# An RWKV attention with a Fourier mix: mirrored row blocks of the fourth batch share their products, x is reversed through DRAM, and the order is written anew

## The chip, the core and the metric

The kernel runs on one core of a Trainium2 chip. The metric is device microseconds of one execution, as a median of several. The engines are TensorE (PE; PEld is its weight load), VectorE (DVE), ScalarE (ACT), GpSimd (POOL) and SyncE (SP, which issues most of the DMAs).

## The reference

Four batches, 768 positions, 8 heads of 48 columns, so d_model is 384. First a linear attention with a decaying state, then a mixing block.

```python
for t in range(S):                       # state: [B, H, 48, 48]
    cur = np.einsum('bhd,bhe->bhde', u[None] * kt, vt)
    y[:, :, t] = np.einsum('bhd,bhde->bhe', rt, state + cur)
    state = wt[:, :, :, None] * state + np.einsum('bhd,bhe->bhde', kt, vt)
x = y, heads side by side                # [4, 768, 384]
mixed = real(fft(fft(x, axis=1), axis=2))
u = x + mixed
un = (u - mean(u)) / sqrt(var(u) + 1e-06)        # per row
out = u + maximum(un @ w_ch1, 0) @ w_ch2         # 384 -> 1536 -> 384
```

The real part of the two transforms has a symmetry: row 768 - t of `mixed`, read backwards over the columns 1 to 383, is row t.

## The kernel before, in words

**Tiling.** Each batch has 6 chunks of 128 rows. `attention` (from L981) works a chunk: it takes the logarithm of w, sums it along the rows with triangular masks on TensorE (L1019; for the first batch, whose chunks go in pairs, L863), makes decayed r and k, transposes them, forms score blocks (L1130, 8 matmuls for a chunk), masks them (L1140) and sums values (L1195); `xb` gets the chunk's x (L1206). `fold` (L1222) adds and subtracts x rows and columns, so that the transform along the sequence needs half the products.

**The mix.** `mix` (L1256) works one batch. TensorE forms the sequence transform for 385 of the rows into `hcs` (L1271, an eviction for each of three column blocks j = 0, 2, 1); the other rows are the mirror of these and are written to `HCR` as a reversed copy with a sign (from L1298). Then each of six row blocks kb gets its products with the column table: `whole` (L1317) takes 3 matmuls with a 384-column table DTM, `parts` (L1326) takes 4 matmuls of 193, 193, 191 and 191 columns and puts the halves together with more vector work. A choice u(b, kb) says how x is added: from the bank by VectorE with `whole` (L1347), by a ScalarE copy and an addition, or with `parts` (L1362, L1365). Then come row statistics (L1376, L1378) and the centred rows `un` as bf16. Three blocks make a half. Its transposition is a choice too: `un_pe` (L1388: 9 transposes on TensorE, L1394, and evictions) or `un_dma` (L1400: one transposing DMA on SP). Then W1 with 12 groups of three matmuls (L1426), relu (L1432 on VectorE, L1434 on ScalarE), W2 with 12 matmuls for a row block (L1446), the result with its residual (L1455), and the write (L1466). The last row block of the fourth batch is split into 256 and 128 columns.

**The start.** `early` (L1477) runs 16 matmuls on a filled part of W1's tile (fill L613); then come the bonus row's matmuls (L713) and, when NW is not 0, NW matmuls on constants (L1522). On ScalarE: the sine tables with one activation table, a load of another (L762), the copy of the bonus row, then the logarithms of the first two chunk pairs. The weights come by POOL's DMAs (W1 at L822, W2 at L827).

**What sets the order.** All operations are first recorded with numbers. `ORDER` lists for each engine the numbers in the order in which the engine issues them; an operation that stands on one of several lists runs on that engine, and a choice is made by listing the operations of one way. `schedule` (L231) follows the lists and gives out PSUM banks, and `emit` (L342) adds semaphore waits. Each engine works its list in order; a waiting operation holds up those behind it, on SP and POOL their DMA issues too. At the end VectorE waits for all writes of the output.

Of the kernel before, what the change touches and what calls it, by code (L numbers as in the profile page):

```python
# [34 lines left out]
NW = 9  # L35

MEANS = (0,)

# [28 lines left out]
    "act": (  # L67
# [15 lines left out]
    "dve": (  # L83
# [17 lines left out]
    "pool": (  # L101
# [49 lines left out]
class _Prog:  # L151
# [190 lines left out]
    def emit(self):  # L342
# [57 lines left out]
        def run(name, eng):  # L400
# [8 lines left out]
            if name == "dve":  # L409
                for s in dcount:  # L410
                    if s.startswith("out"):
                        eng.wait_ge(sems[s], dcount[s])
# [1143 lines left out]
```

## Time and profile before

| | us |
|---|---|
| median of 3 runs (177.77 to 178.5) | 177.8 |
| the profiled execution | 177.74 |
| its span | 175.9 |
| busy: PE / PEld | 171.5 / 114.4 |
| busy: DVE / ACT / POOL | 156.0 / 130.9 / 104.9 |

The span is what the profile shows of one execution; the rest of the time lies around it. Busy times are sums over the span; matmuls are pipelined and their ends are modelled. The chain of waits is followed back from the last instruction.

### The profile page before, as it was taken

Reading aid. Unit: us, or ns where it says so; the run is one execution under the profiler, and the core shown is the slowest. Engines: PE = TensorE matmul, PEld = TensorE weight load, DVE = VectorE, ACT = ScalarE, POOL = GpSimd, SP = SyncE. Lnnn points to the kernel's source line nnn. Section 1 sums busy time; section 2 is a strip of 40 time slices with the busy share of each in tenths; the row PEclk is TensorE's granted clock in tenths of the full one; section 3 lists DMA queues with packets and bytes.
Section 4 is the critical chain, followed back from the end, with each engine's and each line's share of the span. In section 5 each row is a group of like instructions: output and inputs, shape, how many; then the busy total and the mean of one; then the engine's idle time right before and its main releaser. Section 6 shows DMA issues by size and latency. Waiting matters only on the chain.

```text
span 175.9 us, 4537 instructions
## 1 busy us (share of the span) xinstructions
PE 171.5 (97%) x1691; PEld 114.4 (65%) x1691; DVE 156.0 (89%) x374; ACT 130.9 (74%) x320; POOL 104.9 (60%) x145
## 2 busy tenths in 40 slices
PE   6999999999999999999999999999999999999994
PEld 3456767867766667766666667666666776666663
DVE  7999999999999999999999999999899599826253
ACT  2899999999999895999997888797841772454010
POOL 4025279779999466799996929998388334000000
PEclk9999999999999999999999999999999999999999
DMA  5999999899999999999699799969981104240033
GB/s 151 319 270 256 179 216 198 157 178 194 194 180 210 187 207 189 229 237 190 127 202 196 156 204 209 235 88 266 212 203 45 45 6 112 75 130 0 0 134 134
DMA packets 109031, 29.55 MB, mean 168 GB/s; under 512 B 104273, under 2 KB 109010, under 8 KB 109010
## 3 DMA queue, kind: packets, MB, share of 16 engines
q1 hardware_dynamic: 107394, 26.91, 71.8%
q0 software_dynamic: 1616, 2.36, 8.5%
q8 instruction: 13, 0.21, 0.5%
q14 instruction: 8, 0.07, 0.1%
HBM read 23.59 MB, written 4.72 MB: 161 GB/s over the span
## 4 chain that ended last, share of the span: by engine, by line
PE 81%; ACT 14%; DVE 2%; issue 1%; ACTq 0%; DVEq 0%
PE bank L1446 27%; PE bank L1426 27%; PE bank L1317 5%; PE bank L1271 4%; ACT rkt L625 3%; PE bank L1130 3%; PE bank L1195 2%; PE bank L1119 2%; PE bank L998 2%; PE bank L1192 2%; PE bank L1167 1%; ACT vb L616 1%; ACT uf L892 1%; ACT in_w L888 1%; ACT uf L616 1%; PE bank L1019 1%
## 5 line engine op out<-in xcount | busy, mean ns | idle before, releaser
L1426 PE MATMUL bank<-unt,w 128*128 128x384 bf16 x288 | 54.0, 326 | 0.0
L1446 PE MATMUL bank<-w,ht 128*128 128x384 bf16 (+2 forms) x300 | 52.7, 320 | 0.0
L1434 ACT ACTIVATE ht<-bank 128x384 bf16<-128x384 f32 x75 | 35.0, 509 | 13.6 <-PE bank L1426 13.4
L1446 PEld LDWEIGHTS bank<-w,ht 128*128 128x128 bf16 x300 | 27.8, 98 | 15.8 <-DVE ah L1140 0.2
L1426 PEld LDWEIGHTS bank<-unt,w 128*128 128x128 bf16 x288 | 26.8, 98 | 15.2
L1140 DVE TENSOR_TENSOR ah<-bank,msk 128x512 bf16<-128x512 f32 x47 | 30.3, 678 | 0.4 <-PE bank L1130 0.2
L1432 DVE TENSOR_SCALAR ht<-bank 128x384 bf16<-128x384 f32 x21 | 11.2, 552 | 7.7 <-PE bank L1426 7.7
L1455 DVE SCALAR_TENSOR_TENSOR osb<-bank,rstd,uf 128x384 f32<-128x384 f32 (+2 forms) x23 | 13.4, 591 | 4.7 <-PE bank L1446 2.6
L625 ACT ACTIVATE rkt<-bank 128x512 bf16<-128x512 bf16 (+1 forms) x22 | 16.4, 796 | 0.9 <-PE bank L1107 0.7
L602 POOL TENSOR_TENSOR xf<-sd 128x382 bf16<-128x382 f32 (+1 forms) x11 | 10.8, 1002 | 10.2 <-DVE sd L602 7.5
L616 ACT ACTIVATE un<-uf,agg 128x384 bf16<-128x384 f32 x22 | 13.1, 613 | 4.9 <-DVE agg L1378 4.9
L602 POOL TENSOR_TENSOR rkh<-in_k,e 128x384 bf16<-128x384 f32 x15 | 15.0, 1006 | 2.4 <-DVE rk L602 1.5
L602 POOL TENSOR_TENSOR rk<-in_r,in_k 128x384 f32<-128x384 f32 x14 | 13.9, 1002 | 0.8 <-DVE vtd L602 0.8
L602 POOL TENSOR_TENSOR vtd<-in_v,dc 128x384 f32<-128x384 f32 x17 | 14.2, 835 | 0.4 <-DVE dc L1074 0.3
L602 POOL TENSOR_TENSOR rk<-rk,ub 128x384 f32<-128x384 f32 x13 | 13.0, 1005 | 2.0 <-DVE rk L602 2.0
L616 ACT ACTIVATE vb<-in_v 128x384 bf16<-128x384 f32 x23 | 12.9, 569 | 1.2 <-DMA in_v<-in_v_dram 1.2
L1195 PE MATMUL bank<-vb,ah 128*128 128x48 bf16 x192 | 11.2, 183 | 0.0
L1206 DVE TENSOR_TENSOR x<-bank,vtd 128x384 f32<-128x384 f32 x19 | 10.4, 547 | 0.8 <-PE bank L1195 0.7
L1195 PEld LDWEIGHTS bank<-vb,ah 128*128 128x128 bf16 x192 | 9.7, 96 | 1.1 <-issue 0.2
L616 ACT ACTIVATE lb<-in_w 128x384 bf16<-128x384 f32 x18 | 9.7, 542 | 0.1
L1376 DVE BATCH_NORM_STATS2 bst<-uf 128x6 f32<-128x384 f32 x18 | 9.5, 546 | 0.2 <-POOL uf L602 0.2
L1192 PE MATMUL bank<-st,rkt 128*128 128x96 bf16 x80 | 9.7, 204 | 0.0
(208 smaller groups left out, 391.3 us busy)
## 6 DMA issues: line engine op xcount, KB each, us to landing
in_v<-in_v_dram SPq DMA_DIRECT2D x24, 192.0 KB, 3.9
out_dram<-osb SPq DMA_DIRECT2D x23, 192.0 KB, 2.3
in_r<-in_r_dram SPq DMA_DIRECT2D x18, 192.0 KB, 4.2
in_w<-in_w_dram SPq DMA_DIRECT2D x18, 192.0 KB, 3.8
in_k<-in_k_dram SPq DMA_DIRECT2D x18, 192.0 KB, 3.8
in_k<-in_k_dram SPq DMA_DIRECT2D x3, 384.0 KB, 4.5
in_r<-in_r_dram SPq DMA_DIRECT2D x3, 384.0 KB, 4.5
in_w<-in_w_dram SPq DMA_DIRECT2D x3, 384.0 KB, 4.6
```

Of the source, the lines that this page charges most:

```text
L602: return lambda e: e.tensor_tensor(out=o, in0=a, in1=b, op=f)
L616: return lambda e: e.activation(o, a, f, **kw)
L625: {"act": lambda e: e.activation(o(), i(), ACTF.Copy), "dve": lambda e: e.tensor_copy(out=o(), in_=i())}, **kw)
L1140: masked[n].append(op("dve", v_1(512), lambda e: e.tensor_tensor(out=ah[:, x:H:2, :], in0=ps(bk)[:, :].rearrange("p (h t) -> p h t", t=128 ...
L1192: e.matmul(ps(ty)[:, 96 * q:96 * q + 96], rT[:, q, :], s_in[:, q, :], start=not ype, stop=False, skip_group_check=True)
L1195: ins = e.matmul(ps(ty)[:, D * h:D * h + D], ah[:, h, :], vb[:, h, :], start=first and not ype, stop=True, skip_group_check=True)
L1206: op("dve", v_1(DM), lambda e: e.tensor_tensor(out=xb[:, c, 0:DM], in0=ps(ty)[:, 0:DM], in1=vflat, op=ALU.add), r=[ty, ("VTD", n % 4)], w= ...
L1426: ins = e.matmul(ps(t)[:, 0:384], W1[:, m, 256 * (j // 2) + j % 2:256 * (j // 2) + 256:2], unt[:, :, m, :], start=(m == 0), stop=(m == NM ...
L1432: {"dve": lambda e, j=j, t=t, ht=ht: e.tensor_scalar(out=ht[:, j, :], in0=ps(t)[:, 0:384], scalar1=su, scalar2=0.0, op0=ALU.mult, op1=ALU. ...
L1434: "act": lambda e, j=j, t=t, ht=ht: e.activation(ht[:, j, :], ps(t)[:, 0:384], ACTF.Relu, scale=su)},
L1446: ins = e.matmul(ps(t)[:, 0:hi - lo], ht[:, j, 128 * x:128 * x + 128], W2[:, j, lo:hi], start=(j == 0), stop=(j == NJ - 1))
L1455: op("dve", v_1(hi - lo) + 64, lambda e: e.scalar_tensor_tensor(out=o[:, lo:hi], in0=ps(t)[:, 0:hi - lo], scalar=rstd[:, kb:kb + 1], in1=u ...
```

## The change

- `NW` goes from 9 to 0: the matmuls on constants (L1522) are gone.
- `MIRROR = (3,)`: in the fourth batch (b = 3) `HCR` gets 128 reversed columns for each j, and one more copied column, in place of 384. Six row blocks remain, in this order: rows 0 to 127; 128 to 255; 640 to 767; 256 to 383; and then the mirrors of the fourth and of the second, read backwards out of the bank that holds those (`back_bank`), without matmuls. These two banks have 385 columns in place of 384, for which the table DTM gets a column more.
- The mirrored blocks need x with its rows reversed: three SP DMAs write rows 384 to 640 of x to a DRAM scratch `xs3`, and two indirect DMAs on POOL read them back by an index tile `IXI`, made by two iotas on POOL at the start. In the block of row 640 the first row is replaced by row 384 (one column of `HCR`, one row of `xb`); row 640 itself comes with the mirror of the block 128 to 255.
- The results of the mirrored blocks leave by two indirect DMAs on POOL (scatters), which wait for the write of rows 640 to 767; row 384 has its own small write. In the second half the blocks come out in the order 4, 5, 3, and block 3 is the one that is split into 256 and 128 columns.
- VectorE's last waits take in the semaphore of that small write.
- `ORDER` is new for every engine. In it, u(3,0) is `parts`, u(3,1) to u(3,3) are `whole` with VectorE's addition, u(3,4) and u(3,5) are `back_bank`; the first half's transposition of the fourth batch is `un_pe` (before `un_dma`), the second half's stays `un_dma`; one sum of the third batch takes the way with one cumulative matmul (L1019) fewer; the score blocks stand in 18 runs (17 before). The fill for the first 16 matmuls is VectorE's 11th operation (before its first). ScalarE has the first pair's logarithm ahead of the copy of the bonus row. Between the engines, 21 operations go from POOL to VectorE, 14 from VectorE to POOL, 11 from VectorE to ScalarE, 8 from ScalarE to VectorE; the first copy of values goes from ScalarE to POOL. Up to the third of VectorE's table operations (L610) there are 24 operations on its list (before 27). On SP the writes of x to the scratch stand between result writes of the second and third batch; POOL's list ends with the fold, the two gathers, one reversal, one addition and the two scatters.

```diff
-NW = 9
+NW = 0
+MIRROR, T_IND = (3,), 1100
...
-                    if s.startswith("out"):
+                    if s.startswith(("out", "one")):
                         eng.wait_ge(sems[s], dcount[s])
...
-    DTM = sb("dtm", [3, DM], BF16)
+    DTM = sb("dtm", [3, DM + 2], BF16)
+    IXI = sb("ixi", [4], mybir.dt.int32)
...
+        op("pool", 100, lambda e: e.iota(IXI[:, 0:2], [[-128, 2]], base=256, channel_multiplier=-1), w=["IXI"])
+        op("pool", 100, lambda e: e.iota(IXI[:, 2:4], [[128, 2]], base=S * (B - 1) + 512, channel_multiplier=-1), w=["IXO"])
...
+            if b in MIRROR:
+                some = lambda j=j: (HCR[:, j, 256:384], hcs[:, j, 128:0:-1])
...
+        if b in MIRROR:
...
+            xs = XS[b]
+            for q, (lo, n) in enumerate(((0, 128), (128, 128), (256, 1))):
+                op("sp", 620, lambda e, q=q, lo=lo, n=n: e.dma_start(xs[lo:lo + n, :], xb[0:n, 3 + q, 0:DM]),
+                   r=[("X", i, 3 + q)], w=[("XS", b, q)], sem="xs%d_%d" % (b, q), xfer=520 if n > 1 else 100, dma=(1150, 850))
...
+            for y in range(2):
+                op("pool", T_IND, lambda e, y=y: e.indirect_dma_start(
+                    xb[:, 4 - y, 0:DM], None, xs[:, :], bass.IndirectOffsetOnAxis(ap=IXI[:, y:y + 1], axis=0)),
+                   r=[("XS", b, q) for q in range(3 - y)] + ["IXI"], w=[("X", i, 4 - y)], sem="xr%d_%d" % (b, y), xfer=600, dma=(1150, 1300))
...
+            twin, back = mir and kb in (1, 3), mir and kb in (4, 5)
+            row = (0, 128, 256 + 384, 256, 0, 0)[kb] if mir else 128 * kb
+            xk = (0, 1, 5, 2, 3, 4)[kb] if mir else kb
+            t = banks[{4: 3, 5: 1}[kb]] if back else g.tile("f")
...
+                def back_bank(kb=kb, t=t, xk=xk):
+                    op("dve", v_1(DM), lambda e: e.tensor_tensor(
+                        out=uf[:, kb, :], in0=ps(t)[:, DM:0:-1], in1=xb[:, xk, 0:DM], op=ALU.add),
+                       r=[t, ("X", i, xk)], w=[("UF", i, kb)])
...
-                for lo, hi in ((0, DM),) if n < B * NC - 1 else ((0, 256), (256, DM)):
+                for lo, hi in ((0, DM),) if n != B * NC - (3 if B - 1 in MIRROR else 1) else ((0, 256), (256, DM)):
...
+                        if kb > 3:
+                            op("pool", T_IND, lambda e, o=o, kb=kb: e.indirect_dma_start(
+                                out.rearrange("b t d -> (b t) d"), bass.IndirectOffsetOnAxis(ap=IXI[:, kb - 2:kb - 1], axis=0), o[:, :], None),
+                               r=[("OSB", n % 3, lo), "IXO", ("out", b, 2, 0)], w=[("out", b, kb, lo)], sem="outs%d_%d" % (b, kb), xfer=600,
+                               dma=(1150, 1300))
+                            continue
```

## Rows read from the trace of the kernel before

**Rows 1.** The page's busy times: us, share of span, instructions

```profile
PE 171.5 (97%) x1691; PEld 114.4 (65%) x1691; DVE 156.0 (89%) x374; ACT 130.9 (74%) x320; POOL 104.9 (60%) x145
```

**Rows 2.** The chain that ended last, its share of the span by engine

```profile
PE 81%; ACT 14%; DVE 2%; issue 1%; ACTq 0%; DVEq 0%
```

**Rows 3.** Chain of waits in time, 6 to 31 us: start us, us, engine, tile, line

```profile
6.52 1.29 ACT L762
...
8.38 1.47 ACT uf L616 x2
...
11.04 0.41 ACT vb L616
...
29.33 0.94 ACT lb L616 x2
...
30.32 0.34 PE bank L1019
```

**Rows 4.** Windows: length, sum, busy PE, PEld, DVE, ACT, POOL (instructions), PEclk, DMA share, GB/s

```profile
40.00:60.00 20.00, 20.00 (x239) 13.86 (x238) 19.67 (x46) 20.00 (x55) 18.11 (x25) 1.00 1.03 189
...
120.00:140.00 20.00, 20.00 (x189) 13.39 (x188) 17.25 (x36) 12.36 (x32) 12.29 (x13) 1.00 0.72 153
```

**Rows 5.** Timeline, first 10 us: start us, us, engine, line, operation, shape

```profile
1.32 5.30 PE L1479 MATMUL bank<-w 128*128 128x384 bf16 x16 [1.32 <-DVE w L613]
...
7.48 1.64 PE L1522 MATMUL bank<-idw,msk 128*128 128x384 bf16 x9
...
9.26 2.11 PE L863 MATMUL bank<-uf,un 128*128 128x384 bf16 x12
...
1.30 0.11 DVE L613 MEMSET lb<- 128x64 uint32 x1
```

**Rows 6.** Chain of waits, 141 to 150 us

```profile
141.35 0.33 PE bank L1317 x2
...
142.98 0.50 PE bank L1326 x6
...
144.30 0.49 PE bank L1426 x3
...
144.78 5.20 PE bank L1446 x32
```

**Rows 7.** Windows, 139 to 146 us, L1326 alone: busy PE and PEld

```profile
139.00:146.00 7.00, 2.47 (x16) 1.44 (x16) 1.00 0.01 4
```

**Rows 8.** Chain of waits, 105 to 118 us

```profile
105.99 0.33 PE bank L1130 x8
...
114.08 0.22 PE bank L1119 x4
...
117.49 0.55 PE bank L1130 x16
```

**Rows 9.** Timeline of VectorE, batch 3 x sums and additions

```profile
134.81 0.55 DVE L1206 TENSOR_TENSOR x<-bank,vtd 128x384 f32<-128x384 f32 x1
...
141.71 0.56 DVE L1347 TENSOR_TENSOR uf<-bank,x 128x384 f32<-128x384 f32 x1
```

**Rows 10.** DMAs: L827 issue ns; landings of L827, L822, last L1466; transposing DMAs, median

```profile
L827 POOL DMA_DIRECT2D w<-in_moe_w_ch_dram x3: 742/753/757, 44.5 to 56.6; - x3
...
DMA to landing us min/median/max: 4.9/5.4/6.4
...
DMA to landing us min/median/max: 7.6/7.8/8.1
...
DMA to landing us min/median/max: 1.6/1.9/2.0
...
unt<-un SPq DMA_TRANSPOSE x5, 3.3
```

**Rows 11.** The end: chain, then the last operation in the timeline

```profile
167.53 5.89 PE bank L1446 x48
...
173.52 0.35 DVE L1455 SCALAR_TENSOR_TENSOR osb<-bank,rstd,uf 128x128 f32<-128x128 f32 x1 [0.19 <-PE bank L1446]
```

More of the change, by code (lines that the diff above doesn't have):

```diff
@@ L803, in rows @@
                         idn = (IDW if cos or half else NIDW)[p0:p0 + np_, 128 - sh:256 - sh]
-                        src = tab[:, 0:HE] if half == 0 else tab[:, HE - 2:0:-1]
-                        dst = ps(t)[:, 0:HE] if half == 0 else ps(t)[:, HE:DM]
+                        src = tab[:, 0:HE] if half == 0 else tab[:, HE - 2::-1]
+                        dst = ps(t)[:, 0:HE] if half == 0 else ps(t)[:, HE:DM + 1]
                         ins = e.matmul(dst, idn, src, start=(i == 0), stop=(i == len(moves[j]) - 1))
@@ L1298, in mix @@
             g.ctx = ("hcr", b, j)
+            if b in MIRROR:
+                some = lambda j=j: (HCR[:, j, 256:384], hcs[:, j, 128:0:-1])
+                op(None, {"pool": 352, "act": a_sb(128), "dve": v_2(128)},
+                   {"act": lambda e, j=j, sg=sg, some=some: e.activation(*some(), ACTF.Copy, scale=sg),
+                    "dve": lambda e, sg=sg, some=some: e.tensor_scalar(out=some()[0], in0=some()[1], scalar1=sg, scalar2=None, op0=ALU.mult),
+                    "pool": lambda e, sg=sg, some=some: e.tensor_scalar(out=some()[0], in0=some()[1], scalar1=sg, scalar2=None,
+                                                                        op0=ALU.mult)}, port=("dve",),
+                   r=[("HCS", j)] + (["CP"] if j == 1 else []), w=[("HCR", j)])
+                g.ctx = ("mix", b)
+                continue
             op(None, {"pool": 970 if j else 462, "act": a_sb(384), "dve": v_2(384)},
@@ L1306, in mix @@
             g.ctx = ("mix", b)
+        if b in MIRROR:
+            g.ctx = ("mir", b)
+            op(None, {"act": 96, "dve": 70, "pool": 60},
+               {"act": lambda e: e.activation(HCR[:, :, 256:257], hcs[:, :, 384:385], ACTF.Copy),
+                "dve": lambda e: e.tensor_copy(out=HCR[:, :, 256:257], in_=hcs[:, :, 384:385]),
+                "pool": lambda e: e.tensor_copy(out=HCR[:, :, 256:257], in_=hcs[:, :, 384:385])}, port=("dve",),
+               r=[("HCS", j) for j in range(3)], w=[("HCR", j) for j in range(3)])
+            xs = XS[b]
+            for q, (lo, n) in enumerate(((0, 128), (128, 128), (256, 1))):
+                op("sp", 620, lambda e, q=q, lo=lo, n=n: e.dma_start(xs[lo:lo + n, :], xb[0:n, 3 + q, 0:DM]),
+                   r=[("X", i, 3 + q)], w=[("XS", b, q)], sem="xs%d_%d" % (b, q), xfer=520 if n > 1 else 100, dma=(1150, 850))
+            op(None, {"act": a_sb(DM), "dve": v_2(DM), "pool": p_1(DM)},
+               {"act": lambda e: e.activation(xb[0:1, 5, 0:DM], xb[0:1, 3, 0:DM], ACTF.Copy),
+                "dve": lambda e: e.tensor_copy(out=xb[0:1, 5, 0:DM], in_=xb[0:1, 3, 0:DM]),
+                "pool": lambda e: e.tensor_copy(out=xb[0:1, 5, 0:DM], in_=xb[0:1, 3, 0:DM])}, port=("dve",),
+               r=[("X", i, 3)], w=[("X", i, 5)])
+            for y in range(2):
+                op("pool", T_IND, lambda e, y=y: e.indirect_dma_start(
+                    xb[:, 4 - y, 0:DM], None, xs[:, :], bass.IndirectOffsetOnAxis(ap=IXI[:, y:y + 1], axis=0)),
+                   r=[("XS", b, q) for q in range(3 - y)] + ["IXI"], w=[("X", i, 4 - y)], sem="xr%d_%d" % (b, y), xfer=600, dma=(1150, 1300))
+            g.ctx = ("mix", b)
         agg, lnv, rstd = AGG[i], LNV[i], RSTD[i]
+        banks = {}
         su = -1.0 / DM if b in MEANS else -1.0
@@ L1310, in mix, with whole, parts @@
             n = b * NC + kb
-            t = g.tile("f")
-            def whole(kb=kb, t=t):
+            mir = b in MIRROR
+            twin, back = mir and kb in (1, 3), mir and kb in (4, 5)
+            row = (0, 128, 256 + 384, 256, 0, 0)[kb] if mir else 128 * kb
+            xk = (0, 1, 5, 2, 3, 4)[kb] if mir else kb
+            t = banks[{4: 3, 5: 1}[kb]] if back else g.tile("f")
+            banks[kb] = t
+            nw = DM + 1 if twin else DM
+            def whole(kb=kb, t=t, nw=nw, row=row, xk=xk):
                 for j in range(3):
                     def f(e, j=j):
-                        a = 128 * (kb % NP)
-                        return e.matmul(ps(t)[:, 0:DM], (hcs if kb < NP else HCR)[:, j, a:a + 128], DTM[:, j, :],
+                        a = row % 384
+                        return e.matmul(ps(t)[:, 0:nw], (hcs if row < 384 else HCR)[:, j, a:a + 128], DTM[:, j, 0:nw],
                                         start=(j == 0), stop=(j == 2))
-                    op("pe", mm(DM), f, r=[("HCS" if kb < NP else "HCR", j), "DTM%d" % j], w=[t])
-            def parts(kb=kb, t=t):
+                    op("pe", mm(nw), f, r=[("HCS" if row < 384 else "HCR", j), "DTM%d" % j], w=[t])
+            def parts(kb=kb, t=t, row=row, xk=xk):
                 for x, (j, lo, hi, tab, n) in enumerate(((0, 0, HE, DTM[:, 0, 0:HE], "DTM0"), (1, 0, HE, DTE[:, 0:HE], "DTE0"),
@@ L1324, in f @@
                     def f(e, x=x, j=j, lo=lo, hi=hi, tab=tab):
-                        a = 128 * (kb % NP)
-                        return e.matmul(ps(t)[:, lo:hi], (hcs if kb < NP else HCR)[:, j, a:a + 128], tab,
+                        a = row % 384
+                        return e.matmul(ps(t)[:, lo:hi], (hcs if row < 384 else HCR)[:, j, a:a + 128], tab,
                                         start=(x == 0), stop=(x == 3), skip_group_check=True)
-                    op("pe", mm(hi - lo), f, r=[("HCS" if kb < NP else "HCR", j), n], w=[t])
+                    op("pe", mm(hi - lo), f, r=[("HCS" if row < 384 else "HCR", j), n], w=[t])
             if b in MEANS:
@@ L1333, in mix @@
             if b in MEANS:
[L1334 to L1336 removed]
+                op("dve", v_1(DM) + 60, lambda e, kb=kb, t=t, xk=xk: e.scalar_tensor_tensor(
+                    out=uf[:, kb, :], in0=ps(t)[:, 0:DM], scalar=1.0, in1=xb[:, xk, 0:DM], op0=ALU.mult, op1=ALU.add,
+                    accum_out=agg[:, kb, 0:1]), r=[t, ("X", i, xk)], w=[("UF", i, kb), ("SUM", i, kb)])
                 op(None, {"act": a_sb(DM) + 95, "dve": v_2(DM) + 60},
@@ L1344, in mix, with add_bank, add_row, add_parts @@
             else:
-                def add_bank(kb=kb, t=t):
+                def add_bank(kb=kb, t=t, row=row, xk=xk):
                     whole()
                     op("dve", v_1(DM), lambda e: e.tensor_tensor(
-                        out=uf[:, kb, :], in0=ps(t)[:, 0:DM], in1=xb[:, kb, 0:DM], op=ALU.add),
-                       r=[t, ("X", i, kb)], w=[("UF", i, kb)])
-                def add_row(kb=kb, t=t):
+                        out=uf[:, kb, :], in0=ps(t)[:, 0:DM], in1=xb[:, xk, 0:DM], op=ALU.add),
+                       r=[t, ("X", i, xk)], w=[("UF", i, kb)])
+                def add_row(kb=kb, t=t, row=row, xk=xk):
                     whole()
                     op("act", a_ps(DM), lambda e: e.activation(uf[:, kb, :], ps(t)[:, 0:DM], ACTF.Copy), r=[t], w=[("UF", i, kb)])
-                    vec(DM, tt(uf[:, kb, :], uf[:, kb, :], xb[:, kb, 0:DM], ALU.add), r=[("X", i, kb)], w=[("UF", i, kb)])
-                def add_parts(kb=kb, t=t):
+                    vec(DM, tt(uf[:, kb, :], uf[:, kb, :], xb[:, xk, 0:DM], ALU.add), r=[("X", i, xk)], w=[("UF", i, kb)])
+                def add_parts(kb=kb, t=t, row=row, xk=xk):
                     parts()
@@ L1372, in mix, with back_row @@
                 g.ctx = ("u", b, kb)
-                g.choose(("u", b, kb), add_bank, add_row, add_parts)
+                def back_bank(kb=kb, t=t, xk=xk):
+                    op("dve", v_1(DM), lambda e: e.tensor_tensor(
+                        out=uf[:, kb, :], in0=ps(t)[:, DM:0:-1], in1=xb[:, xk, 0:DM], op=ALU.add),
+                       r=[t, ("X", i, xk)], w=[("UF", i, kb)])
+                def back_row(kb=kb, t=t, xk=xk):
+                    op("act", a_ps(DM), lambda e: e.activation(uf[:, kb, :], ps(t)[:, DM:0:-1], ACTF.Copy), r=[t], w=[("UF", i, kb)])
+                    vec(DM, tt(uf[:, kb, :], uf[:, kb, :], xb[:, xk, 0:DM], ALU.add), r=[("X", i, xk)], w=[("UF", i, kb)])
+                g.choose(("u", b, kb), *((back_bank, back_row) if back else (add_bank, add_row) if twin else
+                                         (add_bank, add_row, add_parts)))
                 g.ctx = ("mix", b)
@@ L1435, in mix @@
                    r=[t], w=[("HT", q % 2, j)])
-            for x in range(3):
+            for x in (1, 2, 0) if hf and b in MIRROR else range(3):
                 kb = 3 * hf + x
@@ L1465, in mix @@
                     g.choose(("o", b, kb), out_bank, out_row) if hi - lo == DM else out_bank()
-                    op("sp", 620, lambda e, kb=kb, o=o, lo=lo, hi=hi: e.dma_start(
-                        out[b, kb * 128:(kb + 1) * 128, lo:hi], o[:, lo:hi]),
+                    to, of = out[b, kb * 128:(kb + 1) * 128, lo:hi], o[:, lo:hi]
+                    if b in MIRROR and kb > 1:
+                        if kb > 3:
[3 more added lines that the diff above has]
+                               dma=(1150, 1300))
+                            continue
+                        if kb == 2:
+                            g.ctx = ("one", b)
+                            op("sp", 620, lambda e, o=o: e.dma_start(out[b, 384:385, :], o[0:1, :]),
+                               r=[("OSB", n % 3, lo)], w=[("out", b, kb, 1)], sem="one%d" % b, xfer=100, dma=(1150, 600))
+                            g.ctx = ("o", b, kb)
+                        r0 = 640 if kb == 2 else 256
+                        to = out[b, r0:r0 + 128, lo:hi]
+                    op("sp", 620, lambda e, to=to, of=of: e.dma_start(to, of),
                        r=[("OSB", n % 3, lo)], w=[("out", b, kb, lo)], sem="out%d" % (n % 3), xfer=520, dma=(1150, 600))
@@ L1473, in bass_rwkv6_finch__then__fnet_fourier_mix_kernel @@
     small_constants()
+    XS = {b: nc.dram_tensor("xs%d" % b, [257, DM], FP32).ap() for b in MIRROR}
     g.ctx = "begin"
```

14 lines of the change are left out of this document (6 added, 8 removed), and 139 rows, old and new, of the table ORDER.

## The prediction, made before the change was run

> **What bounds the kernel now.** Start with the summary: TensorE is busy 97% of the span, VectorE 89%, ScalarE 74% [rows 1]. Busy TensorE time is partly modelled, so the chain of waits comes next. It has two parts. Up to 30.3 us it is a serial line of ScalarE work: the sine tables, a table load (6.52), the copy of the bonus row, the logarithms of the first two pairs (8.38), and so on to the logarithms at 29.33, which release a matmul at 30.32 [rows 3]. From there to 173.4 us the chain is TensorE, 81% of the span in all [rows 2]. The windows agree: TensorE is 20.00 of 20 us busy from 40 to 60 and from 120 to 140, while in the later one ScalarE falls to 12.36 and VectorE to 17.25 [rows 4]. So time is won in three ways only: the ScalarE line of the first 30 us gets shorter, TensorE gets fewer columns, or the stretch after its last matmul gets shorter. The profiled execution took 177.74 us with a span of 175.9, so 1.8 us lie outside the span; the median of the runs is 177.8, and I sum against 177.74.
>
> **Part 1, the products removed.** In the fourth batch the old kernel forms six row blocks. Four use four matmuls of about 192 columns (L1326, 16 of them [rows 7]) and two use three of 384 (L1317, 6). On the chain six of the short ones take 0.50 us, 0.083 each, and two long ones 0.33, 0.165 each [rows 6]: 16 x 0.083 + 6 x 0.165 = 2.32 us. The new order keeps the short form for block 0 alone, takes the long form for blocks 1, 2 and 3 (1 and 3 with one more column), and gives 4 and 5 no matmul: 4 x 0.083 + 9 x 0.165 = 1.82. Removed: 0.50 us.
>
> **Part 2, what the new order puts back on TensorE.** The first transposition of the normalised rows in this batch went through a DMA; the new order names the TensorE way: 9 transposes of 128 columns. Four matmuls of that width take 0.22 us on the chain [rows 8], so 9 take 0.50. One sum of the third batch drops its second cumulative matmul of 384 columns (L1019), 0.16 by the long matmul above. The score blocks (L1130) stand in 18 runs instead of 17; two blocks joined take 0.55, one alone 0.33 [rows 8], so one more run costs 2 x 0.33 - 0.55 = 0.11. Sum of parts 1 and 2: -0.50 + 0.50 - 0.16 + 0.11 = -0.05 us. The saving of the shared products is spent on the transposes.
>
> **Part 3, the start.** Nine matmuls on constants go (L1522). They ran 7.48 to 9.12 us, and the first real sums (L863) at 9.26 [rows 5] waited for the logarithms on ScalarE, so the nine cost nothing and their removal gives nothing by itself. What moves the start is the order. The first pair's logarithm now stands ahead of the bonus copy on ScalarE, so it can follow the table load (6.52 + 1.29 = 7.81) directly instead of the copy's end at 8.38 [rows 3], less the 0.1 that an engine needs between two: about 0.5 for the first pair. The second pair's logarithm still comes behind the same three operations and gains only what the table gains. VectorE has three fewer small operations ahead of the table operation that releases the sines; a small one has 0.11 us in the rows [rows 5], and they overlap their neighbours, so 0.1 to 0.3 earlier. One copy of values (0.41 [rows 3]) and one small scaling leave the ScalarE line in the first batch. Together 0.5 to 0.9 off that line. TensorE, which is nearly full already from 9.26, can follow only as far as its own first sums move (0.5 to 0.75). I take -0.6; bounds 0 (VectorE, which gets more work here, holds the line) and -1.3 (all of it, and TensorE's small gaps before 30 us close).
>
> **Part 4, the reversed input.** Rows 384 to 640 of x are written to DRAM by three SP issues and read back reversed by two indirect DMAs on POOL. The last write needs x of chunk 5, ready at 134.81 + 0.55 = 135.4 [rows 9]. Plain writes land 1.6 to 2.0 us after issue [rows 10], so 137.4 at the latest. No row shows an indirect DMA; the nearest are the weight loads on the same software queue: 4.9 to 6.4 us, median 5.4, for 384 KB, 7.6 to 8.1, median 7.8, for 576 KB [rows 10]. The difference, 2.4 us for 192 KB more, gives 5.4 - 2.4 = 3.0 us for 192 KB, my value (an estimate from these rows); bounds 1.6 (fastest plain write) and 8.1 (slowest weight load). So it lands at 140.4, between 139.0 and 145.5. It is wanted by the fourth VectorE operation of the batch's additions; the first stood at 141.71 [rows 9], and three of about 0.5 us lie before it: 143.2. Cover 2.8 us, cost nothing; at 8.1 it is 2.3 late. Behind the waiting gathers on POOL stands the reversal of one table row, wanted about 141; three weight loads were issued from POOL in 742 to 757 ns each [rows 10], so two issues free it at 137.4 + 2 x 0.75 = 138.9. Behind the waiting writes on SP stand four result writes, whose buffers are wanted again 6 us later. Behind the one-row copy on ScalarE, which waits for chunk 3 alone, stand one eviction and the third table's, wanted after 139: no cost.
>
> **Part 5, the hand-over in the batch.** With the transposes on TensorE the first half no longer waits 3.3 us for a DMA [rows 10]; but the old order covers that with 32 matmuls of 5.20 us [rows 6], so nothing is gained. The second half still comes by DMA: 3.3 us behind a result write, under ten groups of L1426 (0.49 each [rows 6], 4.9 us). Slack about 0.4; I take 0, bounds 0 and +0.5.
>
> **Part 6, the scattered output.** Two of the last three row blocks leave by indirect DMAs on POOL. The last VectorE result and its SP write are as before: TensorE ends at 173.42, the last operation starts at 173.52 and takes 0.35 [rows 11], and the write lands 1.6 later [rows 10], about 175.45, 2.03 after TensorE's end. The scatter of block 5 is ready 1.98 us (twelve matmuls of 256 columns and twelve of 128) before that end, plus 0.1 to start and 0.62 for the operation: 1.26 before. So it may take 3.2 us and cost nothing. At 3.0 it is just hidden; at 1.6 wholly; at 4.9, the fastest weight load, it costs 1.7.
>
> The Trainium skill's DMA: Bandwidth & Descriptors, section Anatomy of one DMA, has a fit for this queue, 2.0 us plus bytes over 436 GB/s. For 192 KB that is an estimate of 2.45 us, and the tail would be 0.7 us inside its cover: the same sum. For the 384 KB loads it would be 2.9, where the rows have 4.9 to 6.4 beside other traffic, so here the rows are the safer guide.
>
> A rule that speaks against the change: SBUF — State Buffer, section SBUF: two separate sides (the "DVE blocks DMA" trap), says that VectorE operations in a two-port mode keep POOL from writing its descriptors. By it the gathers, issued while VectorE folds, would go late. The trace disagrees as far as it goes: the three weight loads issued in 0.74 to 0.76 us between 44.5 and 56.6 [rows 10], where VectorE was busy 19.67 of 20 us [rows 4].
>
> Sum: 177.74 - 0.05 - 0.6 + 0 + 0 + 0 = 177.1 us.
>
> **Rivals.** *The scatter ends the kernel (slower).* Place: after TensorE's last matmul. It decides from 3.2 us between POOL's issue and landing. For it: every row of that queue is above (4.9 at best). Against: those moved two or three times the bytes in full traffic, while the tail's plain writes land in 1.6 to 2.0. At 4.9 to 5.4: 177.1 + 1.7 to 2.2 = 178.8 to 179.3.
>
> *The gather comes late (slower).* Place: VectorE's fourth addition, with the rest of the normalisation in its queue and TensorE's transposes behind that. Some 0.7 us lie between that addition's turn and TensorE's running dry, so it decides from 2.8 + 3.0 = 5.8 us by issue and slack together, near 6. At 8.1 VectorE is 2.3 late, less 0.7: +1.6, 178.7. For it: the 576 KB loads. Against: light DMA traffic there.
>
> *The matmuls without work are missed (slower).* The 16 first ones take 5.30 us, 0.33 each, which is 1.2 GHz for 384 columns; the nine take 1.64, 0.18 each, near 2.4 GHz [rows 5] (the granted clock of the windows reads 1.00 [rows 4], so at the start it is the spacing that tells). Between the two stretches TensorE worked on the bonus row. If without the nine the clock rises only after the first sums, those 12, 2.11 us [rows 5], take some 2 us more: 179. Against: the first 16 now wait for a later fill, so with the bonus matmuls they reach to about 8.2 and leave a gap of 0.3 to 0.7.
>
> *All of the start counts (faster).* The ScalarE line gives its 0.9 and TensorE's gaps before 30 us close, 1.2 in all: 177.74 - 0.05 - 1.2 = 176.5. For it: the attention of the second batch is started earlier on ScalarE, so TensorE has more to fill with. Against: TensorE's columns are the same, so no later stage adds to it.
>
> **How the numbers follow.** A measurement of this kernel tells about 0.5% from no change: 176.9 to 178.7 us is "same". The forecast, 177.1, by itself 176.9 to 178.0, has 0.40; the full start 0.38; the scatter 0.11, the gather 0.07, the clock 0.04, all three slower. Faster 0.38, same 0.40, slower 0.22. The range runs from a little under the full start, 175.9, to the scatter at its nearest row, rounded to 178.9; what is left out is the far end of the scatter and the clock.
>
> **What would show it.** Right: the short form four times and the long form nine times in the fourth batch; nine more transposes; the first L863 at 8.5 to 8.8 us; TensorE without idle from 31 us to its end, at about 172.8; the gather landing before its addition. Wrong: idle TensorE around 145 to 150 (gather or second transposition), a last landing of a scatter more than 2.1 us after the last matmul, the first sums at 0.33 spacing, or TensorE's end at 173.4 in spite of an earlier start, which would mean that the new order pays for the start with stalls in the first 60 us.

## The result, and the profile after

The change made the kernel slower: 180.49 us median (179.63 to 180.86) against 177.79 (177.76 to 178.5); the ratio, taken over all executions and not of the medians, is 1.0129, 95% interval [1.0108, 1.0150]. The forecast of 177.1 and its range up to 178.9 missed it. The profiled execution took 180.86 us with a span of 178.7, where the kernel before took 177.74 and 175.9. It is the slowest of the six, and, as is shown below, one of two in which the clock fell: what follows is read from it, and what differs in the other four stands at the end of the account of why the prediction was wrong.

The page's busy times and its chain by engine, after:

```profile
PE 171.4 (96%) x1681; PEld 113.1 (63%) x1681; DVE 157.1 (88%) x377; ACT 133.1 (74%) x327; POOL 102.7 (57%) x143
...
PE 77%; ACT 9%; DVE 8%; issue 2%; POOL 2%; POOLq 1%; ACTq 0%; DVEq 0%
```

Against [rows 1, 2] TensorE is as busy as before with ten matmuls fewer, VectorE's share of the chain is 8% where it was 2%, and POOL, which had none, has 2%. The start of TensorE in the timeline (start us, us, idle before in brackets), and two windows of it (the granted clock is the third number from the end):

```profile
1.96 4.28 PE L1546 MATMUL bank<-w 128*128 128x384 bf16 x16 [1.96 <-DVE w L615]
6.99 0.88 PE L718 MATMUL bank<-osb,vtd 1*128 1x384 f32 x2 [0.76 <-DVE vtd L615]
8.54 3.73 PE L868 MATMUL bank<-uf,un 128*128 128x384 bf16 x12 [0.67 <-ACT uf L618]
```

```profile
7.00:8.00 1.00, 0.87 (x2) 0.25 (x2) 1.00 (x9) 0.91 (x2) 0.51 (x2) 1.00 1.25 278
...
10.00:11.00 1.00, 1.00 (x4) 0.46 (x3) 1.00 (x2) 0.27 (x1) 0.82 (x4) 0.50 1.07 287
```

The first sums do start 0.72 us earlier than in [rows 5] (8.54 for 9.26). But the granted clock fell from 1.00 to 0.50, that is to 1.2 GHz, after TensorE had stood idle for 0.76 and 0.67 us around the bonus row's two matmuls, and the twelve take 3.73 us instead of 2.11. They end about 0.9 us later than before.

In the fourth batch the chain leaves TensorE (start us, us, what):

```profile
138.93 1.04 DVE xf L604 x2
...
140.04 0.80 issue
140.84 1.10 POOL x L1339
...
142.24 0.98 POOL x L1339
...
143.25 0.66 POOL hcr L1309
...
143.92 0.23 ACT hcr L1325
...
144.19 0.50 PE bank L1360 x2
```

VectorE's fold ends at 139.97; 0.8 us later the first gather starts, then the second, then the reversed table row that stands behind them on POOL, a copy, and TensorE, whose matmul starts 0.33 us later than the one ahead of it allowed (the timeline shows 0.17 of that as idle). The end (timeline; then the landings of the two scatters, L1521, and of the last two plain writes, L1533):

```profile
171.82 3.61 PE L1498 MATMUL bank<-w,ht 128*128 128x384 bf16 x33
...
173.58 0.62 DVE L1507 SCALAR_TENSOR_TENSOR osb<-bank,rstd,uf 128x384 f32<-128x384 f32 x1 [0.71 <-PE bank L1498]
173.73 1.09 POOL L1521 DMA_INDIRECT out_dram<-osb,ixi  x1 [24.73 <-DVE osb L1507]
...
175.12 0.98 POOL L1521 DMA_INDIRECT out_dram<-osb,ixi  x1 [0.30 <-issue]
```

```profile
DMA to landing us min/median/max: 2.7/2.7/2.8
...
DMA to landing us min/median/max: 1.7/2.0/2.2
```

Block 5's result is ready at 174.20 and its scatter lands at 175.12 + 2.77 = 177.89; the last plain write, issued at 175.91, lands after 2.2 us at 178.10 and is the last of all. Both are more than 2.4 us behind TensorE's end at 175.43.

So of the 3.12 us between the two profiled executions, 2.01 stand in TensorE's end (173.42 to 175.43), 0.79 behind it inside the span, and 0.32 outside the span.

### The profile page after: what moved, and what is told of

It reads as the page before. It is cut to its first block, busy times and chain, and to the rows that moved or that the text cites. A ratio compares the mean times of both kernels' runs of the same rounds, so it can differ in the third digit from the quotient of the medians.

```text
span 178.7 us, 4523 instructions
## 1 busy us (share of the span) xinstructions
PE 171.4 (96%) x1681; PEld 113.1 (63%) x1681; DVE 157.1 (88%) x377; ACT 133.1 (74%) x327; POOL 102.7 (57%) x143
## 4 chain that ended last, share of the span: by engine, by line
PE 77%; ACT 9%; DVE 8%; issue 2%; POOL 2%; POOLq 1%; ACTq 0%; DVEq 0%
PE bank L1478 24%; PE bank L1498 22%; PE bank L1360 5%; PE bank L1135 4%; PE bank L1276 2%; PE bank L1200 2%; PE bank L868 2%; ACT rkt L627 2%; PE bank L1112 2%; PE bank L1172 2%; PE bank L1197 2%; PE bank L1003 2%; DVE xf L604 1%; PE bank L1446 1%; PE bank L1281 1%
## 5 line engine op out<-in xcount | busy, mean ns | idle before, releaser
L1498 PE MATMUL bank<-w,ht 128*128 128x384 bf16 (+2 forms) x300 | 53.6, 320 | 0.0
L1486 ACT ACTIVATE ht<-bank 128x384 bf16<-128x384 f32 x74 | 34.2, 498 | 11.2 <-PE bank L1478 10.8
L627 ACT ACTIVATE rkt<-bank 128x512 bf16<-128x512 bf16 (+1 forms) x26 | 17.6, 692 | 0.6 <-PE bank L1112 0.3
L604 POOL TENSOR_TENSOR rkh<-in_k,e 128x384 bf16<-128x384 f32 x14 | 13.9, 1004 | 4.7 <-DVE rk L604 2.7
L1521 POOL DMA_INDIRECT out_dram<-osb,ixi x2 | 2.1, 1032 | 25.0 <-DVE osb L1507 24.7
L618 ACT ACTIVATE vb<-in_v 128x384 bf16<-128x384 f32 x22 | 11.8, 570 | 3.8 <-DMA in_v<-in_v_dram 3.8
L618 ACT ACTIVATE un<-uf,agg 128x384 bf16<-128x384 f32 x24 | 14.0, 622 | 0.6 <-DVE agg L1430 0.6
L604 POOL TENSOR_TENSOR rk<-rk,ub 128x384 f32<-128x384 f32 x14 | 13.9, 997 | 0.0
L604 POOL TENSOR_TENSOR rk<-in_r,in_k 128x384 f32<-128x384 f32 x14 | 13.9, 998 | 0.0
L604 POOL TENSOR_TENSOR xf<-sd 128x382 bf16<-128x382 f32 (+1 forms) x8 | 7.9, 1000 | 9.6 <-DVE rk L604 7.0
L1211 DVE TENSOR_TENSOR x<-bank,vtd 128x384 f32<-128x384 f32 x18 | 9.9, 553 | 0.4 <-POOL rk L604 0.3
```

The lines of the kernel that those rows point to most:

```text
L604: return lambda e: e.tensor_tensor(out=o, in0=a, in1=b, op=f)
L618: return lambda e: e.activation(o, a, f, **kw)
L627: {"act": lambda e: e.activation(o(), i(), ACTF.Copy), "dve": lambda e: e.tensor_copy(out=o(), in_=i())}, **kw)
L1211: op("dve", v_1(DM), lambda e: e.tensor_tensor(out=xb[:, c, 0:DM], in0=ps(ty)[:, 0:DM], in1=vflat, op=ALU.add), r=[ty, ("VTD", n % 4)], w= ...
L1486: "act": lambda e, j=j, t=t, ht=ht: e.activation(ht[:, j, :], ps(t)[:, 0:384], ACTF.Relu, scale=su)},
L1498: ins = e.matmul(ps(t)[:, 0:hi - lo], ht[:, j, 128 * x:128 * x + 128], W2[:, j, lo:hi], start=(j == 0), stop=(j == NJ - 1))
```

## The experiments

The time of one kernel varies by 1 to 3 us from run to run, so each is read twice: by its ratio to the kernel before (each with some 6 to 12 runs, beside 6 to 29 of the kernel before) and by the end of TensorE in its profiled execution (173.42 before, 175.43 after). The kernel before had medians of 178.14 to 178.51 beside these runs, not 177.79; the expected times were reckoned from the latter, so they are low by about half a microsecond. Where two kernels share an order, the lag between them is read by comparing the starts of the same matmuls. Line numbers shift a little between kernels: the first sums are L863 to L868, the gathers L1335 to L1339.

**Matmuls without work in the changed kernel, first try.**

```diff
-PSUM_STATE, NE = 1, 16
+PSUM_STATE, NE = 1, 20
...
+            def again(e):
+                for i in range(4):
+                    ins = e.matmul(ps(tw)[:, 0:384], W1[:, 0, 0:128], W1[:, 0, 0:384])
```

> The changed kernel with matmuls without work back: the first run on the filled tile has 20 instead of 16, and four more stand between the bonus row's matmuls and the first sums. Theory 1 (the clock): in the changed kernel the twelve first sums (L868) took 3.75 us at a granted clock of 0.50, in the kernel before 2.11; with TensorE kept at work the granted clock stays 1.00, the twelve take about 2.1, and the time falls by 1.0 to 1.6 us, to 178.9 to 179.5. Theory 2 (the order): the sums become fast but ScalarE's line holds the start anyway, and the time stays within 0.4 of 180.5.

Measured: 180.45 us, 1.0115 [1.0089, 1.0142]. The twelve sums took 2.11 us from 8.67, yet TensorE ended at 174.78, only 0.65 earlier. The planner had moved its waits, and a POOL operation fell beside VectorE (two timelines):

```profile
11.96 1.76 DVE L600 TENSOR_TENSOR rkh<-in_r,in_w 128x768 bf16<-128x768 f32 x1
```

```profile
11.64 1.26 POOL L600 TENSOR_TENSOR rkh<-in_k,uf 128x384 bf16<-128x384 f32 x1 [1.18 <-DMA in_k<-in_k_dram]
```

The same VectorE operation takes 0.96 us where POOL is quiet, and here 1.76. So this run mixes two things and settles neither theory.

**The kernel before without its nine.** `NW = 0`, nothing else.

> The kernel before without its nine matmuls on constants (L1522), all else as it is. Theory 1 (the clock): TensorE stands idle from about 7.5 us to the first sums at 9.26, the granted clock falls to 0.50 and the twelve sums take 3.7 instead of 2.1: 1.0 to 1.6 us more, 178.8 to 179.4. Theory 2 (the order): the nine did nothing, 177.8 as before, within 0.2.

Measured: 179.87 us, 1.0079 [1.0042, 1.0115]; in the profile 179.19, with TensorE's end at 174.84. TensorE in the timeline, then the window over its sums:

```profile
6.44 0.91 PE L709 MATMUL bank<-osb,vtd 1*128 1x384 f32 x2
9.25 3.62 PE L859 MATMUL bank<-uf,un 128*128 128x384 bf16 x12 [1.91 <-ACT uf L612]
```

```profile
8.00:13.00 5.00, 3.75 (x21) 1.97 (x21) 4.38 (x15) 4.04 (x8) 1.37 (x3) 0.67 1.19 291
```

1.91 us of idle in place of the nine, the clock down (0.67 over this window, 0.50 in each microsecond from 10), the same twelve sums 1.51 us longer, TensorE's end 1.42 later. The mean granted clock of an execution is on record for every run: one such fall makes it 0.99, and here it is 0.99 or less in all twelve. The nine were not free to remove: theory 1.

**Splices of the two orders.** The kernel of one order up to a time, the other behind it; four kernels, cut at 127 and at 34 us.

> The old order with its nine matmuls up to about 127 us, then the new one with the mirrored fourth batch. Theory 1 (the clock at the start is most of the loss): the start is as before, and only what is lost in the last batch stays: a wait of 0.3 us for the reversed table row and 0.6 more behind TensorE's last matmul, so 178.4 to 178.9. Rival (the mirrored batch is most of the loss): 179.5 or more. Rival (the mirrored batch by itself pays its 0.5 us on TensorE and its end is hidden): 177.3 to 177.6.

Measured: 182.17 us, 1.0206 [1.0174, 1.0238]. TensorE waits 0.72 us at 129.8 for a transposing DMA and 0.59 at 131.8 for VectorE, neither of which the changed kernel has: the seam costs, and the run says nothing on the mirrored batch.

> The new order without the nine matmuls up to about 127 us, then the old fourth batch, not mirrored, with the old end. Theory 1: the loss at the start stays, the 0.9 us of the last batch goes: 179.2 to 179.8, first sums at half clock. Rival (the mirrored batch is most of the loss): 177.8 to 178.3.

Measured: 180.31 us, 1.0106 [1.0067, 1.0145]; sums of 3.79 us, TensorE's end at 175.84. A loss is there without any mirrored batch, 0.5 more than expected. TensorE is 1.64 us behind the kernel before at 126 us and 2.43 at 134, where it waits 0.61 us for VectorE: 0.79 of the lag comes at this seam.

> The old order with its nine matmuls up to about 34 us, then the new one with the mirrored batch. At 22 us the changed kernel was 1.85 us behind the kernel before in TensorE's work left, at its end 2.0. Theory 1 (the start is the loss; by clock, order, or both): TensorE ends within 0.3 of 173.4, and only the end of the batch adds its 0.6: 178.0 to 178.7. Rival (the new order loses later as well, and the late start only hid it): 179.3 or more.

Measured: 181.13 us, 1.0164 [1.0134, 1.0194]; TensorE waits 0.54 us at 24.4 and ends at 175.50. The time is the rival's. But with its sums at full clock and at 9.26 this kernel is at 40 us as late as the changed one, and the new order does not lose that where it runs without a seam (the run with all four changes, below): a seam again, as at 127 us.

> The new order without the nine matmuls up to about 34 us, then the old one, not mirrored. Theory 1 (the start is the loss): 1.5 to 2.2 us over the kernel before, 179.3 to 180.2, and the lag is there by 22 us. Rival: TensorE catches up, as it is not full before 30 us: 177.8 to 178.5.

Measured: 179.09 us, 1.0042 [1.0014, 1.0070], from 177.61 to 179.87. In its profile (178.02) the first sums took 2.37 us at a clock of 1.00 and TensorE ended at 173.67. So the same start can be harmless, and it was so in this execution. The clock is one thing that varies, not the only one: the three of the twelve executions with a mean clock of 0.99 took 179.14 to 179.87, the nine others 177.61 to 179.51.

**Plain writes for the mirrored blocks.**

```diff
-                            op("pool", T_IND, lambda e, o=o, kb=kb: e.indirect_dma_start(
...
+                            op("sp", 620, lambda e, o=o, kb=kb: e.dma_start(out[b, 128 * kb - 128:128 * kb, :], o[:, :]),
```

> The changed kernel with the two mirrored row blocks written by plain SP writes to rows 384 to 639 instead of the scatters (the rows of the output are then not in their places). The changed kernel's last write landed 2.67 us after TensorE's end, that of the kernel before 2.03. Theory 1 (the scatters cost the end 0.6 us, as they share its last microseconds): 0.4 to 0.7 less, 179.8 to 180.1, last landing 2.0 after TensorE's end. Rival (the end is as long without them): no change, 180.5 within 0.2.

Measured: 180.28 us, 1.0111 [1.0077, 1.0145], 178.84 in its profile, where the span ends 2.65 us after TensorE's end, 0.62 less than after. It carries the changed kernel's start word for word, and shows the other face of it:

```profile
1.95 5.30 PE L1541 MATMUL bank<-w 128*128 128x384 bf16 x16 [1.95 <-DVE w L611]
7.18 1.18 PE L714 MATMUL bank<-osb,vtd 1*128 1x384 f32 x2
8.53 2.29 PE L864 MATMUL bank<-uf,un 128*128 128x384 bf16 x12 [0.17 <-ACT uf L614]
```

```profile
8.00:12.00 4.00, 3.82 (x30) 1.96 (x29) 3.71 (x13) 3.99 (x11) 0.99 (x4) 1.00 1.10 296
```

Here the first sixteen matmuls ran slowly to their end, for 5.30 us instead of 4.28, so TensorE had hardly an idle stretch before the sums, and the clock stayed. The sums are 1.44 us shorter and TensorE ends at 174.05 instead of 175.43. In the changed kernel the filling matmuls became fast at 5.1 us, ended a microsecond sooner, and the idle time after them is what preceded the fall.

**The second table's reversal on ScalarE.** One operation moved from POOL's list to ScalarE's.

> The changed kernel with the second table's reversed columns (the reversal that waits behind the gathers on POOL) made by ScalarE instead. In the changed kernel TensorE stood 0.33 us at 143.9 for it. Theory 1: that wait goes, TensorE ends 0.3 earlier, 180.2. Rival: the gathers, now last, hold VectorE's addition instead, and nothing is gained.

Measured: 180.39 us, 1.0123 [1.0081, 1.0165]: by the time alone, inconclusive. In the profile, at half clock as after (sums 3.62), TensorE has no wait near 144 and ends at 175.00, 0.43 earlier, 0.08 of it from the start and 0.34 at 144. The wait is real and small.

**The matmuls without work again, with the changed kernel's plan unaltered;** alone, with plain writes, with the reversal on ScalarE, and with the old order behind 34 us.

> The changed kernel with 20 first matmuls instead of 16 and four more behind the bonus row's, as in the first try, but with all waits and banks exactly as in the changed kernel (there they had moved, and a POOL operation fell beside VectorE at 11.6 us). Theory 1 (the clock is half of the loss): the granted clock stays 1.00 in every run, the first sums take 2.1 to 2.3 us, TensorE's end comes 1.2 to 1.4 us earlier than in the changed kernel's profile, and the time is 178.8 to 179.4 with little spread. Rival (the start is slow with a full clock too): 180 or more.

Measured: 180.32 us, 1.0114 [1.0082, 1.0146]. The clock stayed, but the twenty took 5.92 us, the sums began at 9.31, and TensorE ended at 174.83. Twenty are too many where they turn fast late: what they save in the clock they spend in length.

> The same, with the two mirrored row blocks written by plain SP writes to rows 384 to 639 instead of the scatters (the rows of the output are then not in their places). Theory 1 (the scatters cost the end 0.6 us): 0.5 to 0.8 under the run beside it, 178.2 to 178.7. Rival: within 0.2 of it.

Measured: 179.85 us, 1.0086 [1.0053, 1.0119]; but its profile has 180.91 and TensorE's end at 176.11, with sums that start at 9.64 and the gather late as in the next run.

> The run with the full clock, with the second table's reversal on ScalarE instead of behind the gathers on POOL. In the profiles this took 0.4 us from TensorE's end. Theory 1: 178.4 to 179.0, 0.3 to 0.5 under the run with the full clock. Rival: within 0.2 of it.

Measured: 180.32 us, 1.0122 [1.0079, 1.0165]. The profile was to gain 0.4 and did not; its chain says why:

```profile
139.38 5.69 DMA x<-xs,ixi
...
145.09 0.56 DVE uf L1413
```

The gather landed 5.69 us after its start; VectorE stood 1.60 us for it, and TensorE 0.64 at 147.16. In the changed kernel's profile the same two gathers took 3.18 and 4.77 us.

> The new order up to about 34 us with the same added matmuls, then the old order, not mirrored: the version that would beat both if the new start by itself is worth its 0.6 us. Theory 1 (with the clock kept, the new start is as long as the old one, since VectorE holds it): 177.7 to 178.1, the kernel before within 0.2. Rival (the forecast's start holds once the clock is kept): 177.0 to 177.4.

Measured: 179.17 us, 1.0048 [1.0026, 1.0069]. Sums from 9.72, for the same reason as above, and TensorE's end at 174.86. Neither theory's number came. No version here beats the kernel before.

**Gathers not held by the planner.** `schedule` lets each POOL operation wait for the last VectorE operation ahead of it that it keeps apart from POOL's; here not the gathers. With the reversal on ScalarE; then with four matmuls ahead of the first sums and the sixteen left; then with plain writes too.

```diff
-                elif last:
+                elif last and not (o.sem or "").startswith("xr"):
                     o.deps.add(last)
```

> The changed kernel with the second table's reversal on ScalarE, and with the two gathers not held until VectorE has ended its fold (a wait that the planner adds to keep POOL and VectorE apart; the data do not need it). In the changed kernel x had landed in DRAM at 138.17 and the first gather started at 140.84. Theory (the gather's landing, 3.1 to 6.0 us after its start, is one of three places that vary): it starts by 139.2, lands before its addition in every profile, TensorE has no wait from 140 to 152, and the time is 0.3 to 0.7 under the changed kernel, 179.8 to 180.2. Rival: the gathers beside VectorE's fold land as late as before, 180.5.

Measured: 180.57 us, 1.0105 [1.0069, 1.0142]. The first gather starts at 139.66, 0.86 us after x has landed; the two land 3.50 and 2.97 us later, and TensorE has no wait from 132 to 152. Beside VectorE's fold the first gather takes 1.42 us on POOL, where it took 1.10 behind it, and it lands no later. The first sums were at half clock (3.71), and the profile has a wait of 0.56 us at 67.8 that the changed kernel's profile does not have: a load of w landed late. TensorE ends at 175.70.

> The same with four matmuls without work between the bonus row's and the first sums, and the first run left at 16. Theory: where the first matmuls turn fast early, the four keep the clock; where they turn fast late, they lengthen the start by up to 0.5. So the granted clock is 1.00 at the first sums, and the time is 178.9 to 179.5. Rival (four do not keep it): as the run beside it.

Measured: 179.81 us, 1.0072 [1.0047, 1.0098]. The sixteen turned fast early, as after, and the four kept the clock: sums of 2.17 us from 8.56. Yet TensorE ended at 174.98. Two loads of w landed late for ScalarE, which waited 0.81 us until 14.03 and 0.9 us ahead of 67, and TensorE lost 0.92 and 0.45 us by them:

```profile
14.03 0.84 ACT L614 ACTIVATE uf<-in_w 128x768 bf16<-128x768 f32 x1 [0.81 <-DMA in_w<-in_w_dram]
```

Neither the changed kernel's profile nor the next run's has these waits, and the next run differs in nothing ahead of the end: executions of one order differ by more than a microsecond without the clock.

> The changed kernel with early gathers, the reversal on ScalarE, four matmuls ahead of the first sums, and plain writes for the mirrored blocks (to rows 384 to 639, so the rows of the output are not in their places). Theory (the four places are all of the loss): TensorE ends within 0.5 of 173.4, 178.0 to 178.5. Rival (the new order loses by itself): 179 or more.

Measured: 179.30 us, 1.0035 [1.0003, 1.0066]; in the profile 178.57, TensorE's end at 173.75, 0.33 after that of the kernel before. The four places together are most of the loss: 1.0129 becomes 1.0035, and of the 0.6 us that are left 0.38 lie outside the span (2.19 us in the median execution for 1.81). Landings of its gathers (L1335):

```profile
DMA to landing us min/median/max: 3.1/3.3/3.5
```

**The forecast's step by itself, in the kernel before.** Two entries of ScalarE's list exchanged, `NW = 6`.

> The kernel before with one exchange: on ScalarE the first pair's logarithm ahead of the copy of the bonus row, as the changed kernel has it, and six matmuls on constants instead of nine, so that they end before the earlier sums. The forecast's step (the first sums move 0.5 and TensorE follows): 177.2 to 177.4. Rival (VectorE holds what follows, as the copy of the bonus row now comes later for it): first sums 0.5 earlier, time 177.6 to 178.0, no change.

Measured: 178.63 us, 1.0016 [0.9987, 1.0045]; in the profile the sums begin at 8.88, 0.38 earlier, and TensorE ends at 173.81, 0.39 later. VectorE's timeline:

```profile
9.15 0.96 DVE L598 TENSOR_TENSOR uf<-uf,ub 128x768 f32<-128x768 f32 x1 [0.71 <-ACT ub L621]
...
16.43 1.22 DVE L1136 TENSOR_TENSOR ah<-bank,msk 128x512 bf16<-128x512 f32 x2
```

The product with the bonus row, 8.42 in the kernel before, now waits 0.71 us for the copy that was put behind the logarithm, and the first masked scores come at 16.43 instead of 16.05. TensorE has made up all but 0.05 us of this at 25 us; the lag comes back where ScalarE's logarithms wait for POOL, and stays to the end:

```profile
29.71 0.94 ACT L612 ACTIVATE lb<-in_w 128x384 bf16<-128x384 f32 x2 [0.51 <-POOL lb L609]
...
30.71 0.34 PE L1015 MATMUL bank<-lb,nle 128*128 128x384 bf16 x1 [0.43 <-ACT lb L612]
```

## Why the prediction was wrong

**Part 3 is the step that failed, twice.** "Their removal gives nothing by itself" was wrong in sign: the nine matmuls were TensorE's work between the bonus row and the first sums, and without them the granted clock fell: in all twelve executions of the old order, in two of six of the changed kernel. In the kernel before that costs 1.42 us of TensorE's end; in the changed kernel the same code ends 1.38 earlier in the execution that kept the clock (174.05, with plain writes) than in the one that lost it (175.43). The rival named this mechanism and its price, 2 us, nearly right (1.4 to 1.6 on the sums), and gave it 0.04. The reason for so little, that the later sixteen with the bonus matmuls would reach to 8.2, assumed that they run at 0.33 each to their end. In the profile of after they became fast on the way and left 0.76 us of idle. With this start as it is, 17 of 42 executions of six kernels have a mean clock of 0.99; with four matmuls put back ahead of the sums, none of 60 is below 0.997. In the profiles the clock fell in the four kernels where the sixteen turned fast early (5.1 to 5.7 us) and nothing filled the gap behind them, not in the two where they turned fast late, and not in the three where they turned early with the four behind them.

The -0.6 itself did not come either. Sums that begin earlier do not help while VectorE holds the line, and VectorE's next product needs the bonus row that the new order copies later. In the exchange by itself, 1.0016 [0.9987, 1.0045], the profile shows the way: VectorE is 0.37 us late from 13.9 us on, POOL behind it as much, and through POOL the logarithms that stood at 29.33 in [rows 3] (29.71), and TensorE's matmul at 30.32 (30.71). With all else undone the new order still ends 0.33 us later, where the forecast had it 0.65 earlier. That VectorE holds it stood there as the bound of 0, and it was the likelier end.

**Parts 1 and 2 held as far as the runs show.** The long form runs 9 times and the short one 4 times between 139 and 150 us, nine transposes were added, and nothing of the loss lies there. A mirrored batch laid into the old order without a seam was not had, so its own worth stays at the forecast's sum of nothing.

**Part 4: a wait was left out, and the sizes were off.** The gather was taken to start when x had landed, at 137.4, and to land 3.0 us later. x landed at 138.17; the gather started at 140.84, because the planner held it behind VectorE's fold, a wait that the prediction had not looked for, and because 0.8 us pass before the first of two indirect DMAs begins. From start to landing it took 3.0 to 6.0 us in the profiles, and all above 3.5 had two result writes in flight beside them. Of the cover of 2.8 us 1.2 was left in the changed kernel's profile (landing at 144.02, its addition at 145.21), and none where it took 5.69. With the late gather TensorE ended at 174.87, with early gathers and the same clock at 173.75: 1.1 us in such an execution. In the others it is 0.33 for the reversal behind the gathers, which was written down as no cost.

**Part 6: the scatter was mis-sized by half a microsecond.** From the ready result to the landing it took 174.20 to 177.89, 3.69 us against a cover of 3.2 and an estimate of 3.0, of which 0.92 passed before POOL started it, behind block 4's scatter (by the prediction's own terms the cover is 1.26 + 2.03, nearer 3.3). Beside the scatters the last plain write took 2.2 us instead of 1.6, and it landed last. With plain writes the span ends 2.65 us behind TensorE instead of 3.27 and 3.22, and the ratio falls in three pairs by 0.0018 to 0.0037 (0.3 to 0.65 us), each within its noise. That rival, with its place and its cause, came true in part and had 0.11. The Trainium skill's DMA: Bandwidth & Descriptors, section Anatomy of one DMA, whose fit gave 2.45 us, is near the 2.7 to 2.8 from POOL's start to the landing at this quiet end; the 0.92 before that start comes on top, and the 3.0 to 6.0 of the gathers, of the same 192 KB, lie above it.

**Part 5 held:** no wait of TensorE at the second half's transposition.

Added up for the two profiled executions, the changed kernel's against the run with all four changes and that against the kernel before: 1.34 us for the clock (there when the first sums end, and the same at 142 us), 0.34 for the reversal at 144, 0.33 for the order, 0.79 behind TensorE's end, of which plain writes take back 0.62, and 0.32 outside the span. That makes the 3.12 that were measured. Three mechanisms that were each given a small chance as the one cause came together; they should have been added, not weighed against one another.

This is the sum of one execution. The ratio says 2.3 us, and four of the six executions kept the clock (a mean of 0.999 or more): they took 179.63 to 180.61, the two others 180.67 and 180.86. Without the 1.34 the sum gives 179.5, close to the fastest. So the clock is the largest term of that profile, but it is not in the median; what made the other three of the four up to 1.1 us slower is in no profile of this kernel. Two things of that size were seen in the others: a gather that landed 5.69 us after its start (1.12 us of TensorE's end) and late loads of w (0.92 and 0.45).

What stays open: the shares of these in the four executions, the 0.3 us outside the span, which all kernels with both the new start and the mirrored batch show (2.1 to 2.2 us for 1.8), and why the first matmuls turn fast at different moments in different executions.

## What to carry to other kernels

A stretch of matmuls on constants can be cover for the clock of those behind it, as it was here: price its removal by the next matmuls at half speed, and look whether whatever is to fill its place could itself end sooner. Before an operation is put ahead of another on one engine, look who waits for the one put behind; here it was the engine that held the line. An indirect DMA is to be priced from the ready data to the landing, with what its engine's order and the planner put ahead of it: 3.7 us for 192 KB at a quiet end, up to 6.8 with 0.8 for its start in a busy place. And a profile is one execution: look at the clock of the others before its largest term is taken for the loss.

## What was not expected of the hardware

The filling matmuls turn from 0.32 to 0.16 us each at different moments in executions of the same code (after 5.1 us, or not before their end at 7.2), and the granted clock column reads 1.00 in both pieces; it shows the fall at the first sums, not the slow beginning. The Trainium skill's TensorE: Matmul & The Clock Gate, section Part 1: The HAM clock gate (the "warmup" mystery), says that the number of slow first matmuls differs between runs of one kernel; these traces agree, with about ten in one and all sixteen in the other. A VectorE operation of 0.96 us took 1.76 beside a POOL operation on tensors.
